# Eight homes for the result tiles in a windowed-attention and gated-MLP kernel, and two constants of its planner

## The chip, the cores and the metric

The kernel runs on one core of a Trainium2 chip. The metric is the device time of one execution in microseconds. Times of the kernel before: 208.35, 211.0 and 208.52 us, median 208.52. A profile comes from one execution of its own.

A core has five engines that run their own instruction streams in order and wait for each other with semaphores: TensorE (PE, matmuls; its weight loads are listed apart as PEld), VectorE (DVE), ScalarE (ACT), GpSimd (POOL) and SyncE (SP). Here POOL and SP mostly issue DMAs. PE writes to PSUM only; ACT or DVE bring a result from there to SBUF.

## The reference

Attention over a window of 128 keys and 4 "sink" keys, then a multiplicative MLP, in float32:

```python
B, H, S, D = 4, 8, 768, 64          # batch, heads, sequence, head size
keep = is_sink | in_window          # key < 4, or 0 <= query - key < 128
a = softmax(where(keep, q @ k.T / sqrt(D), -1e9))
x = (a @ v) as [3072 tokens, 512]
h = ((x @ w1) * (x @ w2)) @ w3      # 512 -> 1024, 1024 -> 1024
out = h @ w_out                     # 1024 -> 512, float32 [3072, 512]
```

## The kernel before

**Stages.** Everything is in bf16 with float32 sums in PSUM. Since nothing stands between `w3` and `w_out`, the kernel first multiplies them to `w3o` (1024x512): blocks of `w3_sb` are transposed on PE (`fold_w3`, L344) and multiplied with `w_out` (`fold_mm`, L374). After that `w3_sb`, 8 rows of 1024 bf16 per partition, is not read again.

For each of the four batches the sequence is cut in six blocks of 128 tokens, or three steps `t` of 256. Per step:

- keys and queries are brought to `kT` and `qT`. For batches 0 and 1 PE transposes them (`transposes`, L202, tile `tp`) and DVE copies them (L205). For batches 2 and 3 (`XPOSE`) SP issues DMA transposes (L211);
- four score units, one for each pair of heads `r` (`scores`): matmuls `sc` (L256), exponential on ACT `ex` (L261), mask on DVE `am` (L265). They are started in pairs, `r` = 0, 1 and 2, 3;
- four value units (`values`): matmuls `av` (L287), then on DVE the reciprocal `rec` (L291) and the scaled rows `xn` (L294). The sinks come in through `vp` (L226, one for each batch, from the first value block) and `sp` (L237, for steps 1 and 2);
- `xn` is transposed to `xT`: on PE for batches 0 and 1 (`xt`, L303, copied by ACT at L307), by DMA transposes on SP for batches 2 and 3 (L314, two for each step).

The MLP of a batch follows in chunks of tokens (256 for batch 0, 384 after that). `gate` makes 8 column blocks; each has two halves `pg` of four matmuls (L327). ACT copies the first half (`a_sb`, L334), DVE multiplies it with the second (`ab`, L331). `project` makes one result of 128 tokens x 512: 8 matmuls `po` (L385), a copy by ACT to SBUF (`o_sb`, L389), and a write of 256 KB to HBM that SP issues (L392). There are 24 results, six for each batch; the last one is made in two halves, with one write from ACT's queue. `o_sb` comes from the pool `work`, which has three buffers, so that the copy of a result waits until the write of the third result before it has landed.

**Loads.** SP loads nine pieces of `w3` and `w_out` first. All else is loaded by POOL in a fixed order: parts of `w3`, keys, queries and values of batch 0 in six blocks, `w1` and `w2`, then batches 1, 2 and 3 in blocks of k, q, v (L105). At most eight of POOL's loads are under way; the ninth is issued when the first has landed.

**The order.** All engines run an order that a planner in the kernel's source writes when the program is built (`manual_schedule`). Each unit is a task with stages (an engine and an assumed time for each), tasks that it must follow, loads that it needs, and a priority. The planner walks through a model of time and picks for PE the task that can start soonest (`pe_pick`), then by priority; stages on ACT, DVE and SP enter a queue and are taken by their time. What it picks is what the engines do, in this order, whatever times the chip then needs. Between POOL's in-order issue, SP's in-order queue (writes, key and query transposes, `xT` transposes) and the four PSUM buffers of the pool `ps_mm` (used by `tp`, `vp`, `sp`, `av`, `xt`, `pg`, `po`), an operation that waits holds back those behind it.

Two inputs of the planner matter here. `service` (L404) gives for each load an issue time and a duration, from which `landings` works out when it arrives; a task is not planned ahead of its loads' arrival. `PACE` (L566) is, by batch, the least distance in modelled us between the starts of two score pairs.

```python
return [(0.87, 0.845 + (0.9 if i[0] in XPOSE and x != "v" else 0.0), [(x, i[0], kb)])
        for kb in range(i[1], i[2]) for x in "kqv"]
```

```python
if kind == "sc" and k["slots"] == 2:
    busy = max(0.0, free["act"] - free["pe"]) + sum(q[2] for q in queue["act"])
    est = max(est, free["pe"] + busy - BACKLOG, last_sc + (PACE[k["name"][1]]))
```

Of the kernel before, what the change touches and what calls it, by code (L numbers as in the profile page):

```python
# [21 lines left out]
def kernel(  # L22
# [13 lines left out]
    nc = tc.nc  # L36
    FP32 = mybir.dt.float32
# [7 lines left out]
    P = 128  # L45
    NP = H // 2
    NB = S // P
# [3 lines left out]
    KFF = DF // P  # L51

    CHUNKS = [[(256 * i, 256 * i + 256) for i in range(3)]] + [[(0, 384), (384, 768)]] * (B - 1)
    XPOSE = (2, 3)
# [7 lines left out]
    work = ctx.enter_context(tc.tile_pool(name="work", bufs=3))  # L62
# [11 lines left out]
    w3_sb = wp.tile([P, KFF, DF], BF16, name="w3_sb")  # L74
# [306 lines left out]
    def project(b, m, n0, n1):  # L381

        po = ps_mm.tile([P, n1 - n0], FP32, tag="mm", name="po")
        for kk in range(KFF):
            nc.tensor.matmul(po[:], ab[b][:, kk, m * P:(m + 1) * P], w3o[:, kk, n0:n1],  # L385
                             start=(kk == 0), stop=(kk == KFF - 1))
        yield
        o_sb = work.tile([P, n1 - n0], FP32, tag="o_sb", name="o_sb")
        nc.scalar.copy(o_sb[:], po[:])  # L389
        yield  # L390
        t0 = b * S + m * P
        (nc.scalar if n0 else nc.sync).dma_start(out=out[t0:t0 + P, n0:n1], in_=o_sb[:])  # L392
        yield

    def keep_busy(n):
# [7 lines left out]

    def service(what, *i):  # L404
        if what == "qkv":
            return [(0.87, 0.845 + (0.9 if i[0] in XPOSE and x != "v" else 0.0), [(x, i[0], kb)])
                    for kb in range(i[1], i[2]) for x in "kqv"]
        if what == "w3":
            return [(0.75, 1.3 * (i[2] - i[1]), [("w3", i[0], h) for h in range(i[1], i[2])])]
        if what == "wo":  # L410
            return [(0.81, 0.65 * (i[1] - i[0]), [("wo", x, 0) for x in range(i[0], i[1], 2)])]
        return [(0.8, 1.34 * (i[1] - i[0]), [(w,) + (n,) for n in range(i[0], i[1])]) for w in ("w1", "w2")]

    def landings(RAW=2.0, POOL=3.0, DGE=1.6, RAMP=(0.33, 0.64, 0.66, 0.9)):

        queues = {"sp": [(RAW, 1.31, 1.0, [("raw",) + x[:3]]) for x in raws],
                  "pool": [(gen, us, 1.9, keys) for x in order for gen, us, keys in service(*x)]}
        left = {n: [us for _, us, _, _ in q] for n, q in queues.items()}
        at = {n: 0 for n in queues}
# [118 lines left out]
    for b in range(B):  # L538
        for c, (t0, t1) in enumerate(CHUNKS[b]):
            last_t = (t1 - 1) // 256  # L540
            us = 0.01 + 0.65 * (t1 - t0) / 384
            for dt in range(KFF):
                n = dt * P // 256
                pr = 1000 + 200 * b + 10 * c + dt
                war = [("p", b - 2, NB - 1)] if b >= 2 else []
                task(("g", b, c, dt, 0), pr + 0.5, gate(b, c, dt, 0), [("pe", us), ("act", 0.2 + us / 2)],
                     ([("xd", b, last_t, 0), ("xd", b, last_t, 1)] if b in X_XPOSE else
                      [("xt", b, NP - 2, last_t)]) + war, [("w1", n), ("w2", n)], "mm",
                     [("g",) + gates[-2] + (1,)] if len(gates) > 1 else [])
                task(("g", b, c, dt, 1), pr, gate(b, c, dt, 1), [("pe", us), ("dve", 0.23 + us / 2)],  # L550
                     [("g", b, c, dt, 0)], ring="mm", half=True)
                gates.append((b, c, dt))
            for m in range(t0 // P, t1 // P):
                for n0 in (0, DM // 2) if (b, m) == (B - 1, NB - 1) else (0,):
                    n1 = n0 + DM // 2 if (b, m) == (B - 1, NB - 1) else DM
                    task(("p", b, m) + ((n0,) if n0 else ()), 1300 + 200 * b + m + n0 / 1000,
                         project(b, m, n0, n1),
                         [("pe", 1.75 * (n1 - n0) / DM), ("act", 0.6 * (n1 - n0) / DM), ("act", 0.1) if n0 else ("sp", SP_US)],
                         [("g", b, c, KFF - 1, 1), *[folded(i) for i in range(KFF)]], ring="mm")
# [3 lines left out]
    MARGIN = {"av": 0.3}  # L563

    YIELD = {"g": 0.0, "av": 0.0, "sc": 0.4, "tdk": 1.5, "tdq": 1.5}
    PACE = [0.0, 4.0, 5.0, 5.0]  # L566
    last_sc = 0.0
    START, WARM_UNTIL = 1.2, 40.0
    BACKLOG = 1.6
# [12 lines left out]
    def pe_pick():  # L582
        best = None
        for k in tasks.values():
# [16 lines left out]
# [3 lines that stand above are left out]
            wait = est - free["pe"]  # L604
# [110 lines left out]
```

## Time and profile before

| | |
|---|---|
| median of three runs | 208.52 us |
| the profiled execution, its own time | 208.02 us |
| its span, from the first to the last instruction | 206.3 us |
| mean granted TensorE clock | 0.990 |
| busy: PE, PEld, DVE, ACT, POOL | 193.7, 120.2, 113.6, 108.3, 79.5 us |
| result copies `o_sb` (L389) | 25, 14.2 us busy |
| their writes (L392) | 24 from SP, 1 from ACT |

The page gives busy time by engine, the span in 40 slices (busy share in tenths, and the granted PE clock), the chain of work that ended last, and groups of equal instructions. Answers from the trace add who waited for whom, a timeline of each engine, and busy times in stretches of the span. A matmul's listed duration overlaps the next one's, so lengths of PE work are read from the chain, where each piece ends as the next begins.

### The profile page before, as it was taken

To read this page: it belongs to the slowest core of one execution; us is meant where nothing else is said; L and a number is where in the kernel's file an instruction comes from. 1 tells how busy PE (TensorE), PEld (TensorE's weight loads), DVE (VectorE), ACT (ScalarE), POOL (GpSimd) and SP (SyncE) were. 2 spreads that over 40 slices of the span, in tenths; PEclk is the share of its full clock that TensorE was granted. 3 is DMA by queue.
4 is the path that set the end of the run, shared out by engine and by line. 5 is a ranking of instruction groups with operands and counts; after the bars stand their busy time and mean duration, and the time that the engine had idled before them with its cause. 6 is when DMAs were issued, how large, how long until landed. Compare 5 with 4: busy or idle time off the path is not lost.

```text
span 206.3 us, 4542 instructions
## 1 busy us (share of the span) xinstructions
PE 193.7 (94%) x1799; PEld 120.2 (58%) x1811; DVE 113.6 (55%) x261; ACT 108.3 (53%) x182; POOL 79.5 (39%) x107
## 2 busy tenths in 40 slices
PE   7999899979999999959799999999999999999993
PEld 2445556967876885536456655656665566554442
DVE  3754488845886675426667763677778244430000
ACT  2333567734854885447565656666665333323332
POOL 5969967669999843824653000000000000000000
PEclk9999999999999999979999999999999999999999
DMA  4999999999999999999999995601111420002334
GB/s 160 382 377 152 164 158 197 195 157 154 155 152 176 173 144 112 183 190 178 155 129 155 157 127 125 209 2 29 25 29 25 137 69 2 0 0 113 147 152 150
DMA packets 105301, 28.35 MB, mean 137 GB/s; under 512 B 95168, under 2 KB 99776, under 8 KB 105280
## 3 DMA queue, kind: packets, MB, share of 16 engines
q0 software_dynamic: 79648, 12.33, 87.8%
q1 hardware_dynamic: 25488, 15.60, 33.5%
q8 instruction: 14, 0.23, 0.5%
q10 hardware_dynamic: 144, 0.13, 0.2%
q14 instruction: 7, 0.06, 0.1%
HBM read 29.36 MB, written 6.29 MB: 173 GB/s over the span
## 4 chain that ended last, share of the span: by engine, by line
PE 67%; DMA 24%; POOL 4%; issue 2%; SPq 1%; ACT 0%; ACTq 0%
PE pg L327 34%; PE po L385 18%; DMA w_sb<-in_moe_w_dram 8%; DMA vN<-in_v_dram 7%; PE av L287 6%; DMA kN<-in_k_dram 5%; PE sc L256 5%; DMA ab<-in_moe_w_out_dram 4%; PE tp L202 2%; POOL qN L105 1%; SPq L152 1%; POOL vN L105 1%; POOL kN L105 1%; POOL w_sb L108 1%; PE sp L237 1%
## 5 line engine op out<-in xcount | busy, mean ns | idle before, releaser
L327 PE MATMUL pg<-xT,w_sb 128*128 128x384 bf16 (+1 forms) x576 | 92.5, 311 | 0.0
L327 PEld LDWEIGHTS <-w_sb 128*128 128x128 bf16 x576 | 53.6, 98 | 25.7 <-issue 2.5
L331 DVE TENSOR_TENSOR ab<-a_sb,pg 128x384 bf16<-128x384 f32 (+1 forms) x72 | 36.6, 509 | 27.6 <-PE pg L327 23.6
L334 ACT COPY a_sb<-pg 128x384 f32<-128x384 f32 (+1 forms) x72 | 32.0, 445 | 37.3 <-DVE ab L331 18.0
L261 ACT ACTIVATE ex<-sc 128x1024 bf16<-128x1024 f32 (+1 forms) x48 | 45.1, 956 | 6.5 <-PE sc L256 6.3
L385 PE MATMUL po<-w3o,ab 128*128 128x512 bf16 (+1 forms) x192 | 43.0, 370 | 0.4
L265 DVE TENSOR_TENSOR am<-ex,maskt 128x1024 bf16<-128x1024 bf16 (+1 forms) x48 | 30.4, 641 | 7.5 <-ACT ex L261 7.4
L385 PEld LDWEIGHTS <-ab 128*128 128x128 bf16 x200 | 18.9, 98 | 19.6 <-issue 0.3
L389 ACT COPY o_sb<-po 128x512 f32<-128x512 f32 (+1 forms) x25 | 14.2, 569 | 29.3 <-PE po L385 23.3
L105 POOL DMA_DIRECT2D qN<-in_q_dram x24 | 21.8, 908 | 8.4 <-DMA vN<-in_v_dram 7.3
L105 POOL DMA_DIRECT2D kN<-in_k_dram x24 | 22.0, 916 | 7.8 <-DMA qN<-in_q_dram 5.6
L105 POOL DMA_DIRECT2D vN<-in_v_dram x24 | 21.9, 911 | 7.9 <-DMA kN<-in_k_dram 6.6
L294 DVE TENSOR_TENSOR xn<-av,rec 128x256 bf16<-128x256 f32 x48 | 20.4, 425 | 1.7
L287 PE MATMUL av<-vN,am 128*128 128x65 bf16 x352 | 20.1, 193 | 0.0
L287 PEld LDWEIGHTS <-am 128*128 128x128 bf16 x352 | 17.2, 98 | 3.4 <-issue 0.5
L291 DVE RECIPROCAL rec<-av 128x4 f32<-128x4 f32 x48 | 8.7, 181 | 18.9 <-PE av L287 18.5
L256 PE MATMUL sc<-qT,kT 64*128 64x128 bf16 (+1 forms) x256 | 13.9, 238 | 0.0
L287 PE MATMUL av<-vs,es 128*128 128x130 bf16 x64 | 12.8, 222 | 0.0
L256 PEld LDWEIGHTS <-kT 64*128 64x128 bf16 x256 | 8.2, 94 | 5.5 <-issue 4.0
L399 PE MATMUL pz<-ksbd 128*128 128x512 bf16 x27 | 8.2, 447 | 1.3 <-DVE ksbd L162 1.3
L374 PE MATMUL ph<-wo_sb,w3t 128*128 128x512 bf16 x30 | 7.6, 380 | 0.9 <-ACT w3o L378 0.4
L307 ACT COPY xT<-xt 128x512 bf16<-128x512 bf16 x12 | 7.1, 596 | 1.6 <-PE xt L303 1.6
(59 smaller groups left out, 116.9 us busy)
## 6 DMA issues: line engine op xcount, KB each, us to landing
out_dram<-o_sb SPq DMA_DIRECT2D x23, 256.0 KB, 2.3
kN<-in_k_dram POOLq DMA_DIRECT2D x24, 128.0 KB, 8.0
qN<-in_q_dram POOLq DMA_DIRECT2D x24, 128.0 KB, 8.5
vN<-in_v_dram POOLq DMA_DIRECT2D x24, 128.0 KB, 8.3
w_sb<-in_moe_w_dram POOLq DMA_DIRECT2D x9, 256.0 KB, 8.6
ab<-in_moe_w_dram SPq DMA_DIRECT2D x3, 512.0 KB, 6.4
ab<-in_moe_w_out_dram SPq DMA_DIRECT2D x3, 512.0 KB, 7.2
kN<-in_moe_w_dram SPq DMA_DIRECT2D x1, 512.0 KB, 9.2
```

The lines of the kernel that those rows point to most:

```text
L105: nc.gpsimd.dma_start(out=dst, in_=rows(src, b, kb))
L256: nc.tensor.matmul(sc[:, e, c:c + n], kT[b][hp, r, kb * P:(kb + 1) * P], qT[b][hp, r, qb * P:qb * P + n], start=True, stop=True)
L261: nc.scalar.activation(ex[:, :, c0:], sc[:, :, c0:], ACTF.Exp, scale=scale)
L265: nc.vector.tensor_mul(am[:, :, c0:], ex[:, :, c0:], mk)
L287: nc.tensor.matmul(o, lhs, rhs, start=(n == 0), stop=(n == len(todo) - 1), skip_group_check=True)
L291: nc.vector.reciprocal(rec[:], av[:, :, :, D:D + 1])
L294: nc.vector.tensor_mul(xns[b, t][:, :, r, :, :], av[:, :, :, 0:D], rec[:].to_broadcast([P, 2, 2, D]))
L327: nc.tensor.matmul(pg[:], w_sb[:, kk, dt * P:(dt + 1) * P], xT[b][:, kk, tk], start=(kk == 0), stop=(kk == NP - 1))
L331: nc.vector.tensor_mul(ab[b][:, dt, tk], gate_a.pop((b, c, dt))[:], pg[:])
L334: nc.scalar.copy(a_sb[:], pg[:])
L385: nc.tensor.matmul(po[:], ab[b][:, kk, m * P:(m + 1) * P], w3o[:, kk, n0:n1], start=(kk == 0), stop=(kk == KFF - 1))
L389: nc.scalar.copy(o_sb[:], po[:])
```

## The change

Three edits:

1. A result tile is no longer taken from the pool `work`. Result `b * 6 + m` has its home in row `(b * 6 + m) % 8` of `w3_sb`, seen as float32 (a row of 1024 bf16 is 512 float32; a half result takes half of the row). The copy by ACT and the write go to and from there.
2. In the planner's model a key or query load of batches 2 and 3 lasts 1.2 us longer than a plain one, where it was 0.9, and the value load of block 4 of batch 0 lasts 1.3 us longer. All later arrivals move accordingly. Nothing changes in how loads are issued.
3. `PACE` for batch 1 goes from 4.0 to 3.6.

```diff
@@ project @@
-        o_sb = work.tile([P, n1 - n0], FP32, tag="o_sb", name="o_sb")
-        nc.scalar.copy(o_sb[:], po[:])
+        o_sb = w3_sb[:, (b * NB + m) % KFF, 2 * n0:2 * n1].bitcast(FP32)
+        nc.scalar.copy(o_sb, po[:])
         yield
         t0 = b * S + m * P
-        (nc.scalar if n0 else nc.sync).dma_start(out=out[t0:t0 + P, n0:n1], in_=o_sb[:])
+        (nc.scalar if n0 else nc.sync).dma_start(out=out[t0:t0 + P, n0:n1], in_=o_sb)
         yield
@@ service @@
-            return [(0.87, 0.845 + (0.9 if i[0] in XPOSE and x != "v" else 0.0), [(x, i[0], kb)])
+            return [(0.87, 0.845 + (1.2 if i[0] in XPOSE and x != "v" else 1.3 if (x, *i) == ("v", 0, 4, 5) else 0.0), [(x, i[0], kb)])
                     for kb in range(i[1], i[2]) for x in "kqv"]
@@
-    PACE = [0.0, 4.0, 5.0, 5.0]
+    PACE = [0.0, 3.6, 5.0, 5.0]
```

Edits 2 and 3 change nothing but the order that the planner writes. The built program has as many instructions on each engine as before. POOL's order is the same. PE's is the same up to the last key transposes of batch 0, and differs from there to the scores of batch 3; SP's differs from the first writes to the `xT` transposes of batch 3.

## Prediction

> **What bounds the kernel now.** I read the page first: the span, the granted clock and the chain of work that ended last.
>
> ```profile
> span 206.3 us, 4542 instructions
> ...
> PEclk9999999999999999979999999999999999999999
> ...
> PE 67%; DMA 24%; POOL 4%; issue 2%; SPq 1%; ACT 0%; ACTq 0%
> ```
>
> The chain is the PE's own work, with loads beside it, so a microsecond is won only where the PE stands idle or runs slowly. One slice of the clock row is a 7. Second I read busy time by stretch, cut where PE stops (columns: stretch, its length, busy time of PE, PEld, DVE, ACT, POOL, granted clock, DMA share, GB/s).
>
> ```profile
> 44.99:46.81 1.82, 0.00 (x1) 0.01 (x1) 0.03 (x1) 0.35 (x1) 0.53 (x2) 1.00 2.46 152
> 46.81:51.25 4.44, 4.44 (x56) 3.49 (x56) 2.31 (x5) 1.95 (x4) 4.44 (x6) 1.00 2.50 154
> 51.25:63.93 12.68, 12.60 (x157) 9.53 (x158) 10.56 (x26) 7.87 (x13) 12.51 (x16) 1.00 2.67 154
> 63.93:86.23 22.30, 22.20 (x276) 16.00 (x277) 13.97 (x36) 15.90 (x28) 14.70 (x18) 1.00 2.15 152
> 87.60:89.95 2.35, 0.00 (x0) 0.00 (x0) 0.00 (x0) 0.64 (x2) 0.27 (x1) 0.96 1.58 162
> 89.95:93.16 3.21, 3.21 (x16) 1.86 (x16) 1.24 (x2) 1.76 (x4) 1.11 (x2) 0.50 1.49 206
> 93.16:98.35 5.19, 5.18 (x52) 3.01 (x49) 3.48 (x9) 3.86 (x6) 2.13 (x3) 1.00 1.80 178
> 98.35:99.69 1.34, 0.00 (x1) 0.01 (x1) 0.94 (x3) 0.48 (x1) 0.88 (x1) 1.00 2.14 153
> ```
>
> From 45 on there are three holes in PE, 1.82, 2.35 and 1.34 us, and right behind the second one 3.21 us at half clock. Between them PE idles 0.08 us in 12.7 and 0.10 in 22.3. Who ends the holes is in the waits (waiter, releaser: total us, times, longest):
>
> ```profile
> ACT o_sb L389 <- DMA out_dram<-o_sb: 5.8, 2, 4.6
> ...
> PE xt L303 <- ACT o_sb L389: 2.4, 1, 2.4
> ...
> PE tp L202 <- DMA kN<-in_k_dram: 1.8, 1, 1.8
> ...
> PE vp L226 <- DMA vN<-in_v_dram: 1.3, 1, 1.3
> ```
>
> The 2.35 us hole is a chain of two waits: PE waits for ScalarE (ACT) to empty a PSUM buffer, and ACT stands in an `o_sb` copy that waits for an output write to leave one of the three `o_sb` buffers. The timelines of ACT and of SP's queue show why that write is late, and one line of the DMA issues (stretch 81 to 86) how long such a write takes.
>
> ```profile
> 84.15 0.59 ACT L307 COPY xT<-xt 128x512 bf16<-128x512 bf16 x1
> 89.31 0.59 ACT L389 COPY o_sb<-po 128x512 f32<-128x512 f32 x1 [4.57 <-DMA out_dram<-o_sb]
> ```
>
> ```profile
> 75.00 1.19 SPq L211 DMA_TRANSPOSE qT<-qN  x1
> 80.17 1.19 SPq L211 DMA_TRANSPOSE kT<-kN  x1
> 81.46 0.53 SPq L392 DMA_DIRECT2D out_dram<-o_sb  x1
> ```
>
> ```profile
> out_dram<-o_sb SPq DMA_DIRECT2D x3, 256.0 KB, 7.8
> ```
>
> SP works in order. Its transpose at 80.17 had to wait for a key load; the write of the third result stood behind it until 81.46, took 7.8 us, landed at 89.3, and only then could ACT copy the sixth result.
>
> **The change part by part. Eight homes.** No instruction is added or removed: the same 25 copies and 25 writes, with `w3_sb` as their SBUF side. A copy now waits for the write eight results back instead of three. Six results exist up to the end of batch 0, so the 4.57 us wait cannot occur; the copy moves up behind the 84.15 one and what is late next is nothing on ACT, which merely had the PSUM buffers' owners queued behind it (an exponential, a gate copy, an `xT` copy). New waits: in rows 4 to 7 the first copy also waits for w3's load, and the first write of rows 0 to 3 for the casts or loads that filled them, all of it over with the folding of w3, before the first result is made. Gain: the 2.35 us hole and, if the half clock comes from it, half of the 3.21 us behind it, 1.60. Together **3.95**.
>
> [...] The trace has the half clock directly behind the only gap above 2 us and none behind 1.82 or 1.34, so I take 3.95 and keep 2.35 as a case.
>
> **Later arrivals: the first hole.** The model now expects the value load of key block 4 of batch 0, and all loads after it, 1.3 us later. In the order of the changed program three more gate halves (12 matmuls of 128x256) stand ahead of the key transposes that wait at 46.81. Such a dozen takes, in the chain:
>
> ```profile
> 48.26 1.31 PE pg L327 x12
> ```
>
> So 1.31 of the 1.82 us is filled with work that before does later, and 0.5 remains, as the load lands when it did. Does the lead survive the next loads? The last key block of batch 1 is the tightest: issued at 56.37, 6.2 us to landing, thus there at 62.6. Before starts the transposes at 63.93; 1.31 earlier is 62.62, and this block is read by the second half of the eight.
>
> ```profile
> 56.37 0.90 POOL L105 DMA_DIRECT2D kN<-in_k_dram  x1
> ```
>
> ```profile
> kN<-in_k_dram POOLq DMA_DIRECT2D x1, 128.0 KB, 6.2
> ```
>
> It just fits; the lead loses between 0 and 0.2 here. I take **1.31**.
>
> **Later arrivals: the third hole.** This is the sink-value matmul `vp` of batch 3, which stands in PE's order where its load isn't there yet. In the new order it stands further back. What before does between that `vp` and the place where it now stands is this stretch of the chain:
>
> ```profile
> 84.53 15.11 DMA vN<-in_v_dram
> ...
> 99.69 0.41 PE vp L226 x8
> 100.09 0.22 PE xt L303 x4
> 100.31 0.65 PE pg L327 x4
> ...
> 102.42 0.22 PE sp L237 x4
> ...
> 105.86 0.18 PE av L287 x6
> 106.04 1.05 PE pg L327 x6
> ```
>
> All of it from 100.09 to 106.04, 5.95 us, now precedes `vp`, with one gate half more (0.65) and without one `sp` (0.22) and one `av` (0.18): 6.20 us. PE therefore comes to `vp` at 98.35 - 3.95 - 1.31 + 6.20 = 99.29. The load lands at 99.64 whatever PE does, since SP and POOL have as many transfers ahead of it as before. The wait shrinks from 1.34 to 0.40: **0.94**. Sum so far 3.95 + 1.31 + 0.94 = 6.20.
>
> **Transposes and writes on SP.** Here order moves most. In the first part of batch 2 the writes of results 3 to 6 stand up to two transposes earlier. The third write now precedes the sixth transpose (before at 75.00), and waits for its projection, which ended at 78.6:
>
> ```profile
> 77.13 1.46 PE po L385 x6
> ...
> 107.42 0.55 PE sc L256 x12
> ```
>
> With one `av` less ahead of it and 1.31 us earlier that is about 77, so this transpose goes some 2.5 us later. Its reader is the score pair at 107.42 (about 101 now); with 8 to 9 us of landing the cover is over 10 us. Cost nothing; without that cover it would cost the 2.5. Later, the `xT` transposes of batch 2's second pair of blocks move from behind the last key transpose of batch 3 to four positions ahead. Before they went at 122.44 though their input was ready at 119.93:
>
> ```profile
> 119.51 0.42 DVE L294 TENSOR_TENSOR xn<-av,rec 128x256 bf16<-128x256 f32 x1
> ```
>
> ```profile
> 122.44 2.50 SPq L314 DMA_TRANSPOSE xT<-xn  x2
> ```
>
> ```profile
> DMA to landing us min/median/max: 2.4/2.5/7.7
> ```
>
> ```profile
> qT<-qN SPq DMA_TRANSPOSE x1, 8.8
> ```
>
> ```profile
> 129.55 0.65 PE pg L327 x4
> ```
>
> All 6.20 earlier: input 113.73, second issue 115.0, in the time of the loads 7.7 (the slowest `xT`) to 8.8 (a `qT` issued near 113): landed 122.7 to 123.8. The gate that reads it is due at 129.55 - 6.20 = 123.35. So 0 to 0.5 late; I take 0.2, nearer to the `xT` row. Had they stayed behind the loads, this would have eaten most of the gain.
>
> **Closer score units.** The gap of 4.0 us between score pairs of batch 1 is asked as 3.6. The pairs end up about 3.4 to 5.7 us of PE work apart, with the same exponentials. An exponential that is late by less than PSUM covers costs nothing; by the stretches above PE now idles 0.18 in 35 us, so 0 to 1, taken 0.2.
>
> **Sum.** 6.20 - 0.2 - 0.2 = 5.8. Against the profiled execution: span 206.3 to 200.5, its own time 208.02 (1.7 outside the span) to 202.2. The median shown is 208.52, 0.5 above it: **202.7**. From about 130 on both programs issue almost the same list to PE.
>
> **Rivals.** *The half clock isn't the hole's.* Only 2.35 is won there: PE reaches `vp` 1.6 later and waits for nothing, so the 0.40 is saved and 1.2 lost: 203.9. For it: a single occurrence. Against: nothing else idles before 89.95. 0.08.
>
> *The wait moves to the loads.* PE runs ahead by 6 us while the loads come when they did. If the `xT` pair lands 3 us later than I think, the gate waits 3 us and, being a hole above 2.35, costs another 1.6: 207.3. For: in before it landed only as the loads ended. Against: the new place on SP. 0.07.
>
> *ACT becomes the bound in batch 1.* A pair of exponentials arriving late in three of six pairs, 0.9 each with the mean row of 956 ns, gives 205.4. For: closer pairs. Against: ACT is busy 15.9 of 22.3 us. 0.06.
>
> ```profile
> L261 ACT ACTIVATE ex<-sc 128x1024 bf16<-128x1024 f32 (+1 forms) x48 | 45.1, 956 | 6.5 <-PE sc L256 6.3
> ```
>
> *Slower than before: the loads themselves slip.* The same kind of load takes 6.2 us alone and 15.11 with SP's transfers beside it. If writes and transposes that go earlier push vN's landing back, `vp` waits L - 99.29 from a lead of 6.6, and beyond 2.35 us it costs 1.6 more: slower than before from L = 104.3, and 210.2 at L = 106. Against: that needs three more transposes ahead of it, and the count is equal. 0.05. [...]
>
> *The change does nothing:* if three homes never bound, 208. The 4.57 us row excludes it, so it gets no chance of its own.
>
> **How the numbers follow.** Forecast 0.74, rivals 0.08, 0.07, 0.06, 0.05. The lower end takes the unknown costs as zero and the 0.40 as gone: 201.9, and 201.6 for the scatter of the runs. The upper end takes in the first rival and half of the third: 204.9. A difference of 2% (204.3) is about what this measurement tells from none: faster 0.78 (the forecast but for 0.02 of its tail, and 0.06 of the first rival), same 0.17, slower 0.05.
>
> **What would show it.** In the changed profile: no wait of ACT L389 for the output write in batch 1; no 7 in the clock row near 90; a hole of about 0.5 before L202 near 46.8; `vp` at about 99.7 with a wait under 0.5, and 6 us more work before it; the `xT` transposes issued near 114 and gates of batch 2 near 123.5. Wrong would be: a new hole above 2 us with half clock behind it, the loads landing later than 100, or scores of batch 1 with PE idle ahead of them.

## The result, and the profile after

| | before | after |
|---|---|---|
| runs, us | 208.35, 211.0, 208.52, 211.02 | 201.62, 202.38, 201.07, 200.98 |
| median, us | 209.76 | 201.34 |
| profiled execution, its own time and span | 208.02, 206.3 | 201.62, 199.9 |
| mean granted clock | 0.990 | 1.000 |

The ratio is 0.9609, with a 95% interval of 0.9517 to 0.97: faster. The time of 201.34 us lies 0.26 below the low end of the range. The median of before here has a fourth run beside the three shown earlier; in the later comparisons it was 208.2, 208.67 and 208.63. Six more runs of the changed kernel gave 201.67 (201.33 to 202.81).

The page of the changed kernel, span, clock and chain:

```profile
span 199.9 us, 4555 instructions
...
PEclk9999999999999999999999999999999999999999
...
PE 90%; DVE 4%; DMA 3%; ACT 0%; issue 0%
```

The 7 in the clock row is gone, and PE is 90% of the chain where it was 67%. Busy time by stretch, cut where PE stops (columns as in the prediction):

```profile
43.98:46.60 2.62, 2.62 (x27) 2.26 (x25) 1.14 (x3) 1.60 (x4) 2.33 (x3) 1.00 2.43 157
61.80:65.70 3.90, 3.19 (x51) 2.20 (x49) 2.99 (x8) 2.47 (x5) 3.90 (x5) 1.00 2.25 190
65.70:85.36 19.66, 19.66 (x232) 14.28 (x233) 12.08 (x32) 14.05 (x25) 12.80 (x16) 1.00 2.14 163
85.36:99.43 14.07, 14.07 (x148) 8.90 (x149) 10.56 (x27) 10.02 (x17) 6.13 (x7) 1.00 1.76 175
99.43:122.95 23.52, 23.52 (x243) 14.06 (x240) 15.02 (x35) 14.77 (x22) 6.11 (x7) 1.00 1.84 162
```

All three holes of before are closed: the first (1.82 us) in the first row, the second (2.35) and third (1.34) in the fourth. One new place has idle time, 3.90 - 3.19 = 0.71 us between 61.80 and 65.70. Behind it PE isn't idle at all up to 122.95. The chain shows what that place waits for:

```profile
56.03 6.51 DMA kN<-in_k_dram
62.54 0.05 issue
62.59 0.58 PE tp L202 x7
63.16 0.02 issue
63.19 0.69 DVE kT L205
...
64.40 0.69 DVE qT L205
65.09 0.10 DVE rec L291
65.19 0.02 issue
65.21 0.43 DVE xn L294
65.65 0.05 issue
65.69 0.39 PE pg L327 x2
```

It is the last key block of batch 1, and behind it a row of copies on DVE that ends in `xn`. In the timelines of ACT and SP's queue the sixth copy waits for its projection alone, and the third write is issued at 77.94 instead of 81.46:

```profile
84.68 0.58 ACT L389 COPY w_sb<-po 128x512 f32<-128x512 f32 x1 [0.88 <-PE po L385]
```

```profile
77.94 0.34 SPq L392 DMA_DIRECT2D out_dram<-w_sb  x1
78.37 1.24 SPq L211 DMA_TRANSPOSE qT<-qN  x1
```

That write landed 5.8 us later, at 83.75, 0.9 us ahead of the sixth copy. So with three buffers this copy would not have waited either, and the profile alone leaves it open whether the homes did anything.

The two spans differ by 6.4 us: 1.82 for the first hole, 3.95 for the second with its half clock, 1.34 for the third, less 0.71 for the new waits, which is 6.40.

### The profile page after: what moved, and what is told of

The parts are those of the page before. It is cut to its first block, busy times and chain, and to the rows that moved or that the text cites. A ratio compares the mean times of both kernels' runs of the same rounds, so it can differ in the third digit from the quotient of the medians.

```text
span 199.9 us, 4555 instructions
## 1 busy us (share of the span) xinstructions
PE 193.3 (97%) x1811; PEld 120.3 (60%) x1811; DVE 113.0 (57%) x261; ACT 108.6 (54%) x182; POOL 79.0 (40%) x107
## 4 chain that ended last, share of the span: by engine, by line
PE 90%; DVE 4%; DMA 3%; ACT 0%; issue 0%
PE pg L327 42%; PE po L385 19%; PE av L287 7%; PE sc L256 6%; PE pz L399 4%; PE ph L374 4%; DMA kN<-in_k_dram 3%; PE pw L374 3%; PE tp L202 2%; PE tp L344 1%; PE xt L303 1%; PE sp L237 1%; DVE qT L205 1%; DVE kT L205 1%; DVE w3t L349 1%
## 5 line engine op out<-in xcount | busy, mean ns | idle before, releaser
L327 PE MATMUL pg<-xT,w_sb 128*128 128x384 bf16 (+1 forms) x576 | 91.5, 308 | 0.3 <-DVE xn L294 0.3
L385 PE MATMUL po<-w3o,ab 128*128 128x512 bf16 (+1 forms) x200 | 43.6, 371 | 0.0
L389 ACT COPY w_sb<-po 128x512 f32<-128x512 f32 (+1 forms) x25 | 14.2, 569 | 25.1 <-PE po L385 25.0
L399 PE MATMUL pz<-ksbd 128*128 128x512 bf16 x27 | 9.5, 505 | 1.3 <-DVE ksbd L162 1.3
```

What stands on the lines that cost most here:

```text
L327: nc.tensor.matmul(pg[:], w_sb[:, kk, dt * P:(dt + 1) * P], xT[b][:, kk, tk], start=(kk == 0), stop=(kk == NP - 1))
L399: nc.tensor.matmul(pz[:], idle[:, 0:P], idle[:, 0:512], start=True, stop=True)
```

## The experiments

All medians are in us; each kernel ran beside runs of the kernel before on the same chip.

**The homes alone.** Edit 1 by itself, in the old order.

```diff
-        o_sb = work.tile([P, n1 - n0], FP32, tag="o_sb", name="o_sb")
+        o_sb = w3_sb[:, (b * NB + m) % KFF, 2 * n0:2 * n1].bitcast(FP32)
```

> Kernel before with edit 1 alone (eight homes in w3_sb); the order on PE, DVE, ACT, POOL and SP stays that of before. Theory A (the holes are in series, and the third is pinned to a load): the 4.57 us ACT wait for the write and the 2.35 us PE hole go, PE comes to vp of batch 3 at about 94.3 instead of 98.35, and then waits there until the value load lands, at 98.3 to 99.6. That is a hole of 4 to 5.3 us, with some 3.4 us of half clock behind it (1.6 to 1.7 lost). Span 206.5 to 208, so no gain. Theory B (each hole has its own price): span 206.3 - 3.95 = 202.4.

Measured: 209.56, of 205.31, 211.5, 209.65 and 209.47, with granted clocks of 1.0, 0.973, 0.992 and 0.984; before beside it 208.2 (205.21 to 210.41). No gain is shown: the median is 1.4 us higher, and four runs that lie 6 us apart decide little. An estimate from the profile of before, where the clock is 0.50 from 89.75 to 93.16: such a stretch of 3.41 us costs about 1.7 us (half of it) and 0.008 of the mean clock (1.7 of 206 us); by that measure the executions have none, about three, one and two of them. That accounts for part of the spread: the run with one is 4.3 us above the one with none. In the profiled one (205.31, span 203.6) ACT no longer waits for an output write, but the chain and the waits have this:

```profile
82.87 14.10 DMA vN<-in_v_dram
96.96 0.05 issue
97.01 0.41 PE vp L226 x8
```

```profile
PE vp L226 <- DMA vN<-in_v_dram: 3.3, 1, 3.3
```

The second hole is closed and the third has grown from 1.34 to 3.31 us. So 1.97 of the 3.95 us that the homes win are spent again in front of the value load of batch 3, although this load landed 2.7 us earlier here (96.96) than in before (99.64). With a landing as late as before's the wait would be 3.31 + 2.68 = 6.0 us, and nothing of the 3.95 would be left. Of the three slower executions there is no profile.

**The two constants alone.** Edits 2 and 3, with the three buffers of before.

```diff
-            return [(0.87, 0.845 + (0.9 if i[0] in XPOSE and x != "v" else 0.0), [(x, i[0], kb)])
+            return [(0.87, 0.845 + (1.2 if i[0] in XPOSE and x != "v" else 1.3 if (x, *i) == ("v", 0, 4, 5) else 0.0), [(x, i[0], kb)])
-    PACE = [0.0, 4.0, 5.0, 5.0]
+    PACE = [0.0, 3.6, 5.0, 5.0]
```

> The changed kernel with edit 1 undone: o_sb from the pool of three buffers, edits 2 and 3 kept; the order on every engine is that of the changed kernel. Theory A (the homes remove the second hole): the sixth copy waits for the third write again, a PE hole of about 2.3 us near 86 and half clock behind it, 4 us in all: span about 204. Theory B (the new order alone removes it, because the third write now stands ahead of two transposes on SP and landed at 83.75 in the changed kernel, before the sixth copy at 84.68): no wait, span 199.9, like the changed kernel within 0.3%.

Measured: 201.57 (201.49 to 201.78), ratio 0.9692 [0.9641, 0.9743]. That is the changed kernel's time (201.34 and 201.67). No copy waits for a write; all waits of PE from 44 us on are short, the longest of them these:

```profile
PE tp L202 <- DMA kN<-in_k_dram: 0.4, 1, 0.4
...
PE pg L327 <- DVE xn L294: 0.3, 1, 0.3
```

The order alone closes the second and the third hole and all but 0.4 us of the first; here the homes add nothing that can be measured.

**A late third write, with three buffers and with homes.** The constants again, but the SP stage of the third result is held back in the planner, so that its write stands behind the transpose of the fourth key block of batch 2, as in before. Both kernels have the same order.

```diff
-            queue[e].append((at + HOP, YIELD.get(k["name"][0], 0.1), us, k))
+            late = {("p", 0, 2): 5.0}.get(k["name"], 0.0) if e == "sp" else 0.0
+            queue[e].append((at + HOP + late, YIELD.get(k["name"][0], 0.1), us, k))
```

> The same as the run before it, three buffers, but the planner's SP stage of the third result is held back 5 us, so that on SP its write stands behind the transpose that waits for the fourth key block of batch 2, as in the kernel before. Theory B: the write is issued near 82, lands near 89, the sixth copy waits over 4 us, PE has a hole of about 2.3 near 86 and half clock behind it: span about 204. Theory A: the same as the run before it. If both are near 200, the wait is not what made the hole.

> The changed kernel with its eight homes, but with the SP stage of the third result held back 5 us in the planner, so that its write stands behind the key transpose that waits for the 16th key load: the same order as the kernel with three buffers and the late write, which took 202.37 us. Theory A (the homes take away what a late write costs): no wait of ACT for an output write, 201.5 us. Theory B (the 0.8 us come from the moved transposes on SP, not from the result buffers): 202.3 us as with three buffers.

Measured: 202.37 (201.92 to 203.22) with three buffers, 201.54 (201.31 to 201.86) with homes. In the first, ACT waits for a write again, in its list of waits and in its timeline:

```profile
ACT o_sb L389 <- DMA out_dram<-o_sb: 4.5, 2, 2.4
```

```profile
86.53 0.59 ACT L389 COPY o_sb<-po 128x512 f32<-128x512 f32 x1 [2.40 <-DMA out_dram<-o_sb]
```

What it waits for is not the third write. In the order that the planner writes here, the write of the fourth result comes first, then the key transpose, then the write of the third (82.43 in this profile, 78.03 with the constants alone):

```profile
80.70 0.34 SPq L392 DMA_DIRECT2D out_dram<-o_sb  x1
81.14 1.24 SPq L211 DMA_TRANSPOSE kT<-kN  x1
```

The write at 80.70 is thus the fourth result's. It landed at 86.43, and the sixth copy began at 86.53, while the third write landed only at 90.60: the copy took the buffer whose write was first in the order. The wait is about half as long as in before (2.40 us where it was 4.57), mostly since this write landed 5.7 us after its issue, where the one at 81.46 in before took 7.8. It left PE idle for only 0.18 us at its next transpose, and the median is 0.8 higher. With the homes, measured on another chip, the 0.8 is gone. Of it the two profiles (spans 200.7 and 200.0) explain a part: the 0.18, and 0.2 that was lost earlier and has nothing to do with the writes (the last key transposes of batch 1 begin at 62.68, against 62.47 with the homes). So the homes are an insurance: worth nothing with an early third write, and up to 0.8 us with one that is 4.4 us later.

**A hole without a transfer in it.** The changed kernel with five copies on ACT (128x1024, row 6 of `w3_sb` to row 7, not yet in use) ahead of the sixth result copy.

```diff
+        if (b, m) == (0, NB - 1):
+            for _ in range(5):
+                nc.scalar.copy(w3_sb[:, 7, :], w3_sb[:, 6, :])
```

> The changed kernel with five copies of 128x1024 bf16 in dead rows of w3_sb added on ACT ahead of the sixth result's copy, 5 us in all: the hole of before is made again without any DMA wait. Theory A (a PE hole of this length is followed by one half-clock stretch of 3.4 us): PE hole about 2.9 near 86, half clock behind it in most runs, span 199.9 + 2.9 + 1.6 = 204.4. [...]

Measured: 206.2 (204.46 to 206.63, eight runs), 4.5 to 4.9 above the changed kernel's two medians. The five copies took 5.37 us, the sixth result copy started at 89.31 as in the kernel before, PE had a hole of 2.06 us, and by stretches the clock halved behind it:

```profile
84.13:87.55 3.42, 3.42 (x48) 2.35 (x46) 1.12 (x4) 3.32 (x5) 1.44 (x2) 1.00 1.87 186
87.55:90.96 3.41, 1.14 (x6) 0.48 (x5) 0.12 (x1) 3.38 (x5) 0.87 (x1) 1.00 1.38 175
90.96:94.38 3.42, 3.06 (x18) 1.58 (x18) 2.32 (x6) 2.01 (x4) 2.46 (x3) 0.50 2.28 181
```

The span of 204.8 is 4.9 above the changed kernel's: 2.06 for the hole, 1.53 for the half clock (half of the 3.06 busy), 0.48 for a wait of PE during it, and 0.5 since PE came later to the first key transposes in this execution (47.10 against 46.60); 0.3 is not accounted for. Six of the eight runs show a clock of 0.989 to 0.992, two 1.0; these two are the fastest and the slowest, so the half clock isn't all that sets them apart. The half clock thus comes from the hole, whatever makes the hole, but not in each execution.

**Each constant alone, and two of them,** all with three buffers.

> The kernel before with only one line of the change: the value load of block 4 of batch 0 modelled 1.3 us longer. Three result buffers, gap 4.0, key and query loads of batches 2 and 3 as before. In the order that comes out, three gate halves stand ahead of the key transposes that waited 1.82 us, the third result is made some 10 us of PE work earlier and its write goes out ahead of the second transpose on SP, but the sink-value matmul of batch 3 stands only 0.65 us of PE work later than before (5.3 us earlier than in the changed kernel). Theory A (holes in series: what is won ahead of that matmul is lost at it, unless it is moved back too): PE comes to it near 94.1, its load lands at 95.4 to 99.6 as in the six executions seen, so it waits 1.3 to 5.5 us, mostly with half clock behind it: about 206.7 us, 203.5 to 208.5. Theory B (the terms of my sum are independent): the second hole with its half clock and the first hole go, 5.26 us in all: about 203 us, and the wait at the sink-value matmul stays near 1.3 us.

> The kernel before with only the key and query loads of batches 2 and 3 modelled 1.2 us longer than a plain one (0.9 before). Three result buffers. In the order that comes out, the key transposes of batch 0 stand where they stood before (the hole of 1.3 to 1.8 us stays), the third write stands ahead of the seventh transpose on SP, and the sink-value matmul of batch 3 stands 3.8 us of PE work later than before. Theory A (holes in series): PE starts 1.3 us late from the first hole, the short waits at 62 to 66 that the changed kernel has (0.7 us) are gone for it, and it comes to the sink-value matmul near 98.0 with the load landing at 95.4 to 99.6: 202.2 us, 201.9 to 203.5. Theory B (independent terms): second hole with half clock 3.95, most of the third 0.94: 208.2 - 4.9 = 203.3 us. What tells more than the time: under A the first hole of over 1 us is the only one above 0.5 us from 44 us on unless the load comes after 98.5.

> The kernel before with both modelled arrivals of the change, but the score pairs of batch 1 still 4.0 us apart, and three result buffers. The order has the first hole's gate halves as in the changed kernel, an early third write, and the sink-value matmul of batch 3 at 2.1 us of PE work ahead of its place in the changed kernel. Theory A (holes in series): PE comes to it near 97.3, and waits for a load that lands at 95.4 to 99.6: 0 to 2.3 us lost, about 202.4 us; so the closer score pairs are worth up to 1 to 2 us, though I booked them as a cost of 0.2. Theory B (the closer score pairs only cost): 201.4 us, as fast as the changed kernel or 0.2 faster.

> The kernel before with only the least distance of score pairs of batch 1 at 3.6 us instead of 4.0. Three result buffers. In the order that comes out, the third result is written early (second write behind the first transpose), three of the six results of batch 0 are made only after the scores of batch 3, and the sink-value matmul of batch 3 stands 0.7 us of PE work ahead of its place before, 6.7 ahead of that in the changed kernel. Theory A (holes in series): PE comes to it near 93.3 and waits until its load lands at 95.4 to 99.6, 2 to 6 us with half clock behind most of these holes: about 207.5 us, 205.5 to 209. Theory B (independent terms): the second hole and its half clock go, 3.95 us: 204.6 us.

| kernel | median | lowest to highest | before beside it | PE's wait at `vp`, profiled |
|---|---|---|---|---|
| value load later | 207.37 | 206.15 to 209.22 | 208.67 | 3.1 |
| key and query loads later | 203.74 | 203.14 to 206.1 | 208.67 | 1.2 |
| both | 205.25 | 202.44 to 205.84 | 208.67 | 0.6 |
| closer score pairs | 207.27 | 205.97 to 209.46 | 208.63 | 2.1 |
| all three | 201.57 | 201.49 to 201.78 | 208.2 | none |

The first and the last of the single constants came out as holes in series say (206.7 and 207.5 expected, against 203 and 204.6 for independent terms): they close the second hole and pay at `vp`, which they hardly move. (With the closer pairs a later copy, at 124.17, waits 4.30 us for a write; 0.62 of that reaches PE.) With the key and query loads later the median is nearer to the independent terms' 203.3 than to 202.2; the load landed at 99.47, past the 98.5 that the expectation names, so the time doesn't tell the two apart. With both arrivals neither theory holds: three of the four runs are near 205.5, and only the fourth, 202.44, is where theory A has it. The waits and the chain of that kernel show a hole that no other one has:

```profile
PE sp L237 <- DMA qT<-qN: 2.2, 1, 2.2
```

```profile
77.33 17.82 DMA qN<-in_q_dram
95.16 0.02 issue
95.17 8.26 DMA qT<-qN
103.43 0.14 issue
103.56 0.29 PE sp L237 x4
```

A query load of batch 2 took 17.82 us, the transpose on SP behind it went at 95.17 (90.56 in the changed kernel), and PE stood for its result. Why the load takes longer in this order is open. By the medians the constants don't add up: one by one they win 1.3, 4.9 and 1.4 us, the first two together 3.4, all three 6.6. But the second and the pair have four runs each, and these overlap; that the pair is slower than the second alone is not shown.

**Longer still.** Two variants of the changed kernel, with the value load modelled 1.5 and 1.7 us longer instead of 1.3, and the changed kernel beside them.

> The changed kernel itself once more, as the measure for the two variants that run beside it. 201.3 us, 201.0 to 202.4 as in its first four runs.

> The changed kernel with the value load of block 4 of batch 0 modelled 1.5 us longer than a plain one instead of 1.3. In the order that comes out, the key transposes for the last block of batch 1 stand 0.2 to 1.7 us of PE work later, the third result is made early, and the sink-value matmul of batch 3 stays where it is. Theory A (what is left in the changed kernel are the short waits between 62 and 66 us, 0.7 us in all, and they go when the work ahead of them grows): 200.7 us, 0.6 below the changed kernel beside it. Theory B (a chain of other short waits takes their place, as the four-fold scatter of the single steps suggests): within 0.3 us of it, or up to 1 us slower.

> The same with 1.7 us. The sink-value matmul of batch 3 then stands 2 us of PE work later than in the changed kernel, and the xT transposes of the first pair of blocks of batch 2 stand one pair of transposes earlier on SP. Theory A: 200.7 us as with 1.5, since the load was there 1.2 us ahead already. Theory B: within 0.3 us of the changed kernel, or up to 1 us slower.

Measured: 201.67 (201.33 to 202.81) for the changed kernel, 201.18 (199.7 to 201.58) with 1.5, and with 1.7 201.23; one of its six runs took 689.92 us for a reason that nothing here shows, the other five 200.76 to 201.35. In the same stretch as above the kernel with 1.7 has PE busy throughout:

```profile
61.80:65.70 3.90, 3.90 (x46) 2.56 (x45) 2.44 (x5) 2.44 (x5) 3.90 (x6) 1.00 2.22 177
```

The short waits are gone. With 1.5 they are gone too, but 0.95 us are left of the first hole and 0.36 at `vp`. The medians are 0.4 to 0.5 below the changed kernel's, less than the 0.6 expected, and the runs overlap: probably a small gain, not a shown one.

## Why the prediction was right in direction and 1.4 us too high

It expected a net 5.8 us off the span and 202.7; the span lost 6.4, and the median is 201.34. Of the 1.36 us, 0.6 is in the sum, where terms too high and too low partly cancel, and 0.78 in the last step, which is the one that put the forecast's range above the measured time.

**Eight homes: 3.95.** The size was right, and the hole and its half clock went. What failed is that this step gave the hole to the homes ("the 4.57 us wait cannot occur"). The prediction itself said, under transposes and writes, that the third write now precedes the sixth transpose; that alone lands it in time, and it was priced at nothing. The constants alone take 201.57, the homes alone 209.56. Two edits each removed the same wait, and I credited the one that I met first. That the size came out all the same is luck as far as the homes go.

**The first hole: 1.31, with 0.5 left, and 0 to 0.2 lost later.** In the profiled execution nothing was left (1.82 won); the five others with the same order up to that point have 0.40 to 0.67 left, as predicted. The 1.82 was one draw as well: with the homes alone, in the order of before, this hole is 0.83. The loss at the last key block of batch 1 was mis-sized: 0.71. PE was there at 62.27, ahead of the 62.62 forecast, and waited 0.32 for the load, which landed at 62.54 (62.6 forecast). Behind it came 1.9 us of DVE copies that the step didn't price, and PE waited 0.26 for `xn`. The two together are worth 1.11 instead of 1.31.

**The third hole: 0.94, with 0.40 left.** PE came to `vp` at 99.43 (99.29 forecast), and did not wait: 1.34. What failed is "the load lands at 99.64 whatever PE does". It was issued at 82.82 and landed after 15.4 us, by POOL's timeline and the list of DMA issues:

```profile
82.82 0.89 POOL L105 DMA_DIRECT2D vN<-in_v_dram  x1
```

```profile
vN<-in_v_dram POOLq DMA_DIRECT2D x1, 128.0 KB, 15.4
```

That is 98.25. An earlier landing doesn't need the new order: with the homes alone, where POOL's and SP's order is that of before, it landed at 96.96. Over all fourteen profiled executions, of thirteen programs, it landed between 95.42 and 100.26; in the two of the changed kernel itself at 98.25 and 100.26. The 99.64 was one draw from a spread of up to 5 us.

**The `xT` pair, 0.2.** Issued at 113.37 as forecast (113.73); each landed within 7.1 us, below the 7.7 to 8.8 that I took, at 121.06 at the latest. The gate at 122.95 waited for nothing.

**Closer score units, a cost of 0.2.** There is no wait of PE for an exponential. By the medians the sign was wrong as well: without this edit the two other constants take 205.25 (202.44 to 205.84), with it 201.57 (201.49 to 201.78). What it does is move projections, writes and transposes, not only scores.

**The last step: 0.5 added, since the median shown was above the profiled execution.** That difference is real for before; all its later medians lie 0.2 to 0.65 above its profile too. The likely cause, argued and not tested by itself, is the holes: their length follows when loads land, and by the granted clocks (down to 0.976) and the estimate of 0.008 for each, up to three stretches of half clock come on top, while its executions spread over 205.2 to 211.6. Carrying it to a kernel without these holes was the error. The changed kernel's median lies 0.28 *below* its profiled run, and its ten runs spread over 200.98 to 202.81; in the repeat the profiled execution was the slowest of six, 1.14 above the median. The range's low end carried the 0.5 along, 201.6 instead of 201.1, and so missed.

**The rivals.** That the half clock isn't the hole's is refuted by the kernel with the five copies, whose profile has the half clock right behind a hole that no load or write made. No rival happened in the changed kernel; but a wait that moves on to the next load is what the homes alone, the value load alone and the closer pairs alone did.

## What to carry to other kernels

Where PE waits for loads at several places, the holes are in series: closing one brings PE earlier to the next load, where part of the gain is spent waiting (with the homes alone 1.97 of 3.95 us). An edit is worth what is left behind the last load that binds, so follow the new lead through each of them, and ask for each pair of edits whether both remove the same wait.

When a load's landing sets a hole, take its spread over executions (95.42 to 100.26 here), not its one value; and an offset between the profile and the median of one kernel need not carry over to a kernel without its holes (0.2 to 0.65 in before, -0.28 in the changed kernel).

## What was not expected of the hardware

The length of a hole alone does not tell whether half clock follows it. Three kernels have a stretch of 3.41 us at a clock of 0.50 inside the work in their profiles: before (89.75 to 93.16), the value load alone (96.74 to 100.15) and the five copies (90.96 to 94.38, in the rows shown there). With the homes alone and with the closer pairs alone PE has a hole in the same part of the work, and the clock is 1.00 through it and behind it. Busy time and clock around the hole, in before, with the value load alone, with the homes alone and with the closer pairs alone:

```profile
86.33:89.75 3.42, 1.27 (x16) 0.68 (x15) 0.80 (x3) 0.43 (x1) 0.91 (x2) 1.00 1.52 189
89.75:93.16 3.41, 3.21 (x16) 1.86 (x16) 1.24 (x2) 1.97 (x5) 1.31 (x2) 0.50 1.47 214
```

```profile
93.33:96.74 3.41, 0.47 (x3) 0.08 (x1) 1.49 (x5) 0.52 (x2) 2.86 (x4) 1.00 2.33 158
96.74:100.15 3.41, 3.22 (x32) 2.25 (x32) 0.50 (x2) 1.55 (x3) 2.39 (x3) 0.50 2.31 153
```

```profile
91.70:95.12 3.42, 2.00 (x21) 1.14 (x18) 2.10 (x5) 1.94 (x4) 1.59 (x2) 1.00 1.84 190
95.12:98.53 3.41, 1.52 (x24) 1.20 (x25) 0.13 (x1) 1.07 (x2) 2.62 (x3) 1.00 2.12 155
98.53:101.94 3.41, 3.41 (x34) 1.92 (x32) 2.80 (x10) 2.73 (x5) 2.88 (x4) 1.00 2.16 156
```

```profile
92.66:96.07 3.41, 1.70 (x11) 0.80 (x9) 1.58 (x3) 1.63 (x3) 2.41 (x3) 1.00 2.03 154
96.07:99.48 3.41, 2.98 (x42) 2.14 (x44) 1.68 (x5) 1.47 (x3) 1.08 (x2) 1.00 2.40 110
```

The holes of 2.35 us (before), 3.1 us (the value load alone) and 2.06 us (the five copies) have the half clock behind them; those of 3.31 us (the homes alone) and 2.1 us (the closer pairs alone) do not. What decides is not shown by these profiles, nor why the kernel with the five copies has a clock below 1.0 in six of eight executions and 1.0 in two; only one of them was profiled. So in these kernels a hole of 2.06 us was enough for the half clock, and one of 3.31 us did not bring it.
